# Order of five engines planned in eight passes instead of one, in a fused attention and mixer kernel

## Chip, cores and metric

One core of one Trainium2 chip. The metric is the device time of one execution in microseconds (us), lower is better. The kernel before takes 726.40 us (median of three runs, 725.94 to 727.46).

## The reference

Three layers follow each other on an array of 4 batches of 576 tokens with 512 channels: attention over a window of 128 tokens, a mixer with a low-rank product over tokens and a hidden layer of 2048, and a gated layer whose gate mixes tokens. All inputs and outputs are float32.

```python
def _attn_ref(q, k, v):                       # q, k, v: (4, 8, 576, 64)
    scores = scale * np.matmul(q, k.transpose(0, 1, 3, 2))
    mask = (rel >= 0) & (rel < 128)           # rel: distance of the two tokens
    scores = np.where(mask, scores + bias[None], -1000000000.0)
    scores = scores - np.max(scores, axis=-1, keepdims=True)
    attn = np.exp(scores)
    attn = attn / (np.sum(attn, axis=-1, keepdims=True) + 1e-09)
    return np.matmul(attn, v)

def _moe_ref(x, U, V, w_ch1, w_ch2):          # x: (4, 576, 512)
    h = x.transpose(0, 2, 1) @ U @ V
    u = x + h.transpose(0, 2, 1)
    return u + np.maximum(u @ w_ch1, 0.0) @ w_ch2

def _moe2_ref(x, w_in, w_spatial, b_spatial, w_out):
    h = np.maximum(x @ w_in, 0.0)
    u, v = (h[..., :512], h[..., 512:])
    v_n = (v - mean(v)) / np.sqrt(var(v) + 1e-06)
    v_s = np.einsum('ts,bsd->btd', w_spatial, v_n) + b_spatial[None, :, None]
    return (u * v_s) @ w_out
```

## The kernel before

Nothing is issued while the program is written down. Every step (a group of matmuls, an activation, a copy, a transfer) is a `Task` of the class `Plan`: the engines that may do it, its cost on each by a formula (`mm`, `dve`, `act`, `pool_tt`), the tasks it depends on, and a priority `prio`, a number that the author wrote beside the step. At the end `Plan.run` makes one pass forward in time: it takes the engine that is free first, gives it the ready task with the lowest `prio`, notes start and end by the formulas, and goes on. The order in which tasks were taken is the order in which every engine's instructions are then written, and each engine executes its own list strictly in order. The formulas thus set the order, never the time on the chip. A step with two ways (a multiplication on POOL or DVE, a copy on ACT or DVE) goes to the engine that takes it first.

TensorE's steps have a mode: full array (`None`), "quarters" (four matmuls of 64 rows and 64 columns side by side) or "quarter rows". When the mode of a PE task differs from that of the task before it, the plan adds 0.09 to its end.

The work in order of time:

- **Attention.** For each batch and each of four pairs of heads (`heads`, sixteen in all): scores (L911, quarters), the masked minimum on DVE (L922), the exponential on ACT (L927), the scaling by the row sum (L938 for the first batch; L947 on POOL or L949 on DVE for the others, nine a pair), 13 transposes of the weights (L957), copies out of PSUM (L376 on ACT, L377 on DVE), and the product with v (L995, quarters). SP loads q, k and v of each pair (L877, L888).
- **Low-rank mixing** of each batch: transposes of the attention's output (L1022), the product with U (L1038) and with V (L1051), and the sum on DVE (L1056). V's integer words are converted on DVE, and copied by four transfers (L859) of SP into the layout that L1051 wants.
- **Early groups.** The first quarter of the hidden layer, for three groups of 512 tokens (`early_group`), is woven into the attention: `first_of` (L505 to L507, 512 columns, PSUM bank `f1`) and `second` (L544 to L546, bank `acc`, four output blocks e = 0 to 3 one after the other). `collect` (L554) adds a block to the result and frees the bank. The ring `r_acc` has the one bank `acc`; the ring `r_a4` has the three `sc` banks of the scores and `acc`.
- **Rest of the hidden layer**: `first_of` and `second` with 384 columns, then `seven_group` (L766 to L768, L544 to L546), which makes each product of two-by-two blocks with seven multiplications. I call this the dense stage.
- **Gated layer** for each batch: `values_of` (L1273 to L1275), `gates_of` (L1349 to L1351, three banks X, Y and Z for each of i = 0 and 1, emptied by L1356 and L1360), the token mixing (L1393 to L1398), `outputs_of`, and the transfer of the result.

Of the kernel before, what the change touches and what calls it, by code (L numbers as in the profile page):

```python
# [11 lines left out]
F32 = mybir.dt.float32  # L12
# [128 lines left out]
    __slots__ = ("eng", "cost", "emit", "ways", "prio", "deps", "succ", "left", "before", "start", "lat", "port", "mode")  # L141


class Plan:


# [35 lines left out]
    def dma(self, p, n, emit, r=(), w=(), prio=0):  # L182

        self.add("SP", max(0.5, p * n * 4 / 235e3), emit, r=r, w=w, prio=prio, lat=2.6)

    def run(self):
        seq = {t: i for i, t in enumerate(self.tasks)}
        engines = sorted({e for t in self.tasks for e in t.ways})
        free = dict.fromkeys(engines, 0.0)
        port, mode = 0.0, None  # L190

        waiting = {e: [] for e in engines}
        ready = {e: ([], []) for e in engines}
# [26 lines left out]
        order = []  # L220
        while True:
# [14 lines left out]
            at, e = best  # L236
# [3 lines left out]
            if e in rival and choice:  # L240
# [3 lines left out]
                queue = min(choice)  # L244
                if queue is ready[e][1] and theirs and theirs[0][0] < queue[0][0]:
                    choice.remove(queue)
                    if not choice:
# [3 lines left out]
                        e = other  # L251
# [2 lines left out]
            queue = min(choice, default=None)  # L254
            if queue is None:
                continue
            t = heapq.heappop(queue)[2]
            t.start = at
            t.eng, t.cost, t.emit = t.ways[e]
            end = at + t.cost  # L260
            if e == "PE":
                end += 0.09 * (t.mode != mode)
                mode = t.mode
# [7 lines left out]
                if not s.left:  # L271
                    offer(s)
        assert len(order) == len(self.tasks)
        for t in order:
            t.emit()


def mm(n, m=128):
# [20 lines left out]
def tile_kernel(ctx, tc, qT, kT, v, U, V, w1, w2, w_in, wspT, bsp, w_out, bias, out):  # L299
# [212 lines left out]
        P.add("DVE", dve(n), lambda: nc.vector.scalar_tensor_tensor(  # L512
            out=hl.ap(), in0=src(), scalar=0.0, in1=f32(hh.ap()), op0=ALU.max, op1=ALU.subtract), r=r + [hh], w=[hl], prio=prio)

    def early_group(t0, n, wts, prio, evac):

        hs, ls = split_u(t0, n, evac, True)
        hid = []
        w = 512 // n
        for i in range(0, 4, w):  # L520
            f1 = r_f1.new([128, w, n], F32)
            for j in range(w):
                wt = wts[i + j][0]
                P.add("PE", 12 * mm(n), lambda f1=f1, j=j, wt=wt: first_of(f1[:, j], wt, hs, ls),
                      r=[p for x in hs + ls for p in x[2]] + [wt.part(0), wt.part(1)], w=[f1], prio=prio)
            hh, hl = r_h.new([128, w, n], F32R), r_h.new([128, w, n], F32R)
            leave_one(f1.ap, w * n, hh, hl, r=[f1], prio=evac)
            hid += [(hh, hl, j) for j in range(w)]
        for e in range(0, 4, w):
            es = tuple(range(e, e + w))  # L530
            acc = r_acc.new([128, w, n], F32)
            for i in range(4):
                second(wts, hid, i, es, acc, n, prio)
            collect(t0, n, es, acc, True, evac)
# [556 lines left out]

    done = 0
    for n in K["early"]:
        early_group(done, n, parts_w[0], 1e4 + done / 256, K["evac"])
        done += n

    r_xd, r_hl, r_c, r_t = (Ring(in_chan, tag, n, [end_att]) for tag, n in (("xd", 20), ("hl", 8), ("c", 6), ("t", 3)))
# [414 lines left out]
```

## Time and profile before

| What | Value |
|---|---|
| median of three runs | 726.40 us |
| the profiled execution | 726.64 us |
| its span | 724.84 us |
| PE busy | 708.5 us (98%) |
| DVE busy | 557.7 us (77%) |
| ACT busy | 331.7 us (46%) |
| POOL busy | 87.1 us (12%) |
| granted TensorE clock | 1.00 in every slice |
| chain that ended last, by engine | PE 87%, DVE 8%, ACT 2% |

PE's matmuls overlap, so a busy share near 100% can hide a slower pace: the pace is read from the starts of consecutive matmuls in the timeline. The span is 1.80 us shorter than the execution.

### The profile page before, as it was taken

The page shows a single profiled execution, that of the slowest core. Times are in us where ns is not written, and L with a number is a line of the kernel's source. Part 1 is how long each engine was busy: PE and PEld are TensorE (multiplying, and loading weights), DVE is VectorE, ACT ScalarE, POOL GpSimd, SP SyncE. Part 2 cuts the span into 40 slices and gives each one's busy share as a digit, 9 for nine tenths or more (in the row PEclk, how much of TensorE's full clock was granted, in tenths as well). Part 3 has the DMA queues.
Part 4 walks back from the last instruction along what each step waited for, and adds up shares of the span by engine and source line. Part 5 has one row for each costly group of instructions (what it writes and reads, how often), then busy time and mean ns, then how long its engine had stood idle before and what let it go on. Part 6 is the DMA issues. An engine that isn't in the chain of part 4 may idle for free.

```text
span 724.8 us, 14526 instructions
## 1 busy us (share of the span) xinstructions
PE 708.5 (98%) x5472; PEld 644.2 (89%) x5472; DVE 557.7 (77%) x1547; ACT 331.7 (46%) x904; POOL 87.1 (12%) x121
## 2 busy tenths in 40 slices
PE   7989999999999999999999999999999999999997
PEld 5657778778799999999999999999889898898896
DVE  5989997774597999999885997975599768368360
ACT  6977656564452635346042361432354524324212
POOL 1254221120400000000000000010342100100000
PEclk9999999999999999999999999999999999999999
DMA  9574312300064145727173253547631201100102
GB/s 266 184 256 139 97 49 82 92 16 2 1 213 164 56 164 190 229 88 244 50 233 100 90 207 114 161 135 266 211 140 42 74 26 50 64 11 1 58 1 73
DMA packets 53525, 84.07 MB, mean 116 GB/s; under 512 B 7504, under 2 KB 37712, under 8 KB 53456
## 3 DMA queue, kind: packets, MB, share of 16 engines
q1 hardware_dynamic: 53168, 82.86, 34.8%
q8 instruction: 43, 0.70, 0.4%
q10 hardware_dynamic: 288, 0.30, 0.1%
q14 instruction: 26, 0.21, 0.1%
HBM read 60.56 MB, written 22.28 MB: 114 GB/s over the span
## 4 chain that ended last, share of the span: by engine, by line
PE 87%; DVE 8%; ACT 2%; POOL 1%; issue 1%; DMA 1%; SPq 0%; ACTq 0%; POOLq 0%
PE sc L546 8%; PE sc L544 8%; PE sc L545 8%; PE at L767 6%; PE at L766 6%; PE at L768 6%; PE at L995 3%; PE sc L911 2%; PE at L957 2%; PE sc L1273 2%; PE sc L1275 2%; PE sc L1274 2%; PE acc L544 2%; PE acc L546 1%; PE acc L545 1%; DVE p L922 1%
## 5 line engine op out<-in xcount | busy, mean ns | idle before, releaser
L546 PE MATMUL sc<-hl,wa 128*128 128x384 f32 x320 | 108.8, 340 | 0.0
L544 PE MATMUL sc<-h,wa 128*128 128x384 f32 x320 | 107.5, 336 | 0.0
L545 PE MATMUL sc<-h,wa 128*128 128x384 f32 x320 | 107.4, 336 | 0.0
L927 ACT ACTIVATE p<-p,nmax 128x192 f32<-128x192 f32 (+1 forms) x144 | 61.7, 432 | 18.4 <-DVE nmax L922 18.2
L773 DVE TENSOR_TENSOR c<-at,c 128x384 f32<-128x384 f32 x90 | 50.0, 555 | 14.4 <-PE at L768 10.7
L766 PE MATMUL at<-xd,wa 128*128 128x384 f32 x180 | 60.8, 338 | 0.0
L768 PE MATMUL at<-xd,wa 128*128 128x384 f32 x180 | 60.8, 338 | 0.0
L767 PE MATMUL at<-xd,wa 128*128 128x384 f32 x180 | 60.8, 338 | 0.0
L546 PEld LDWEIGHTS sc<-hl,wa 128*128 128x128 f32 x320 | 60.1, 188 | 0.1
L544 PEld LDWEIGHTS sc<-h,wa 128*128 128x128 f32 x320 | 60.1, 188 | 0.0
L545 PEld LDWEIGHTS sc<-h,wa 128*128 128x128 f32 x320 | 60.0, 187 | 0.0
L811 DVE TENSOR_TENSOR y<-sc,y 128x384 f32<-128x384 f32 (+1 forms) x96 | 41.5, 456 | 24.0 <-PE sc L546 23.7
L922 DVE CUSTOM_DVE_ANT_0 p<-sc,bias 128x192 f32<-128x192 f32 (+1 forms) x144 | 40.8, 329 | 10.8 <-DMA bias<-in_bias 5.1
L376 ACT CAST wa<-st 128x256 fp32r<-128x256 f32 (+1 forms) x62 | 27.8, 475 | 31.6 <-DVE st L425 16.4
L911 PE MATMUL sc<-kr,qr 64*64 64x192 f32 (+2 forms) x576 | 33.3, 327 | 3.8 <-DMA kr<-in_kT 3.7
L778 ACT ACTIVATE h<-c 128x384 fp32r<-128x384 f32 x54 | 28.4, 526 | 14.1 <-DVE c L773 14.0
L563 POOL TENSOR_TENSOR t<-y 128x288 f32<-128x288 f32 x1 | 1.5, 1463 | 272.7 <-DVE y L811 272.7
L766 PEld LDWEIGHTS at<-xd,wa 128*128 128x128 f32 x180 | 33.8, 188 | 0.1
L767 PEld LDWEIGHTS at<-xd,wa 128*128 128x128 f32 x180 | 33.8, 188 | 0.0
L768 PEld LDWEIGHTS at<-xd,wa 128*128 128x128 f32 x180 | 33.8, 188 | 0.0
L957 PEld LDWEIGHTS at<-ident,p 128*128 128x128 f32 x208 | 23.4, 142 | 11.4 <-issue 2.8
L957 PE MATMUL at<-ident,p 128*128 128x128 f32 x208 | 31.6, 284 | 1.8 <-DVE p L949 0.8
(364 smaller groups left out, 1965.7 us busy)
## 6 DMA issues: line engine op xcount, KB each, us to landing
wa<-in_w SPq DMA_DIRECT2D x32, 512.0 KB, 5.0
xd<-formsa SPq DMA_DIRECT2D x24, 192.0 KB, 3.9
qr<-in_qT SPq DMA_DIRECT2D x15, 288.0 KB, 4.4
kr<-in_kT SPq DMA_DIRECT2D x15, 288.0 KB, 4.3
vr<-in_v SPq DMA_DIRECT2D x16, 256.0 KB, 3.6
raw<-in_w_in SPq DMA_DIRECT2D x8, 512.0 KB, 3.8
out<-h SPq DMA_DIRECT2D x15, 256.0 KB, 2.0
keptu<-raw SPq DMA_DIRECT2D x14, 256.0 KB, 2.4
```

Of the source, the lines that this page charges most:

```text
L544: nc.tensor.matmul(o, wt[:, 0, 0, c], hh[:, j], start=i == 0 and x == 0, stop=False, skip_group_check=True)
L545: nc.tensor.matmul(o, wt[:, 1, 0, c], hh[:, j], start=False, stop=False, skip_group_check=True)
L546: nc.tensor.matmul(o, wt[:, 0, 0, c], hl[:, j], start=False, stop=i == len(wts) - 1, skip_group_check=True)
L766: nc.tensor.matmul(o.ap(), wh()[:, k], xh.ap(), start=start and k == 0, stop=False, skip_group_check=True)
L767: nc.tensor.matmul(o.ap(), wl()[:, k], xh.ap(), start=False, stop=False, skip_group_check=True)
L768: nc.tensor.matmul(o.ap(), wh()[:, k], xl.ap(), start=False, stop=k == 1, skip_group_check=True)
L773: P.add("DVE", dve(N3), lambda: nc.vector.tensor_tensor(out=out.ap(), in0=ps_.ap(), in1=sb.ap(), op=ALU.add), r=[ps_, sb], w=[out], prio=0)
L811: P.add("DVE", dve(m), lambda acc=acc, dst=dst, s=s, m=m, o=o: nc.vector.tensor_tensor(out=dst[:, s : s + m], in0=acc[:, 0, o : o + m], in ...
L911: nc.tensor.matmul(s[o : o + 64, c0 : c0 + k1 - k0], qr[d, 64 * t : 64 * t + 64], kr[d, k0:k1], start=True, stop=True, skip_group_check=True)
L922: nc.vector.tensor_tensor_reduce(out=o(), in0=s[:, c0 : c0 + nk], in1=bias_t[:, pair, t % 2, 192 - nk :], scale=-0.125, scalar=BIG, op0=AL ...
L927: nc.scalar.activation(out=o(), in_=o(), func=AF.Exp, scale=-1.0, bias=nmax[:, sl, t : t + 1], accum_out=sums[:, sl, t : t + 1])
L957: P.add("PE", 0.109, lambda pt=pt, n_=n_, s0=s0: nc.tensor.transpose(pt[:, n_ - s0], p[:, n_ * 128 : n_ * 128 + 128], ident), r=[p.part(t) ...
```

## The change

`Plan.run` now makes eight rounds. In each, `forward` does what the one pass did; then `latest` walks the same tasks backward in time on the engines that they were given, and writes into each task's `prio` the negative of its distance from the end, so that the next round's forward pass takes first what must start first. The written priorities count in the first round alone. The plan with the smallest planned end of the eight is emitted. On PE, a ready task of the mode that is running is preferred to any other. The last early group's blocks e = 2 and 3 are summed in the ring `r_a4`, that is in two `sc` banks.

```diff
+PASSES = 8
@@ class Plan
+    def latest(self):
+        ahead, left = dict.fromkeys(self.tasks, 0.0), {t: len(t.succ) for t in self.tasks}
+        engines = sorted({t.eng for t in self.tasks})
+        free = dict.fromkeys(engines, 0.0)
+        waiting, ready = {e: [] for e in engines}, {e: [] for e in engines}
+
+        def offer(t):
+            heapq.heappush(waiting[t.eng], (ahead[t], -t.start - t.cost, self.seq[t], t))
+
+        for t in self.tasks:
+            if not left[t]:
+                offer(t)
+        for _ in self.tasks:
+            at, e = min((free[e] if ready[e] else max(free[e], waiting[e][0][0]), e) for e in engines if ready[e] or waiting[e])
+            while waiting[e] and waiting[e][0][0] <= at:
+                heapq.heappush(ready[e], heapq.heappop(waiting[e])[1:])
+            t = heapq.heappop(ready[e])[2]
+            free[e] = at + t.cost
+            t.prio = -free[e]
+            for d in t.deps:
+                gap = self.SAME.get(e, 0.13) if d.eng == e else self.CROSS
+                ahead[d] = max(ahead[d], free[e] + gap + d.lat)
+                left[d] -= 1
+                if not left[d]:
+                    offer(d)
+
     def run(self):
-        seq = {t: i for i, t in enumerate(self.tasks)}
+        self.seq = {t: i for i, t in enumerate(self.tasks)}
+        plans = []
+        for _ in range(PASSES):
+            order = self.forward()
+            plans.append((max(t.start + t.cost + t.lat for t in order), len(plans), [(t, t.eng, t.cost, t.emit, t.start) for t in order]))
+            self.latest()
+        for t, t.eng, t.cost, t.emit, t.start in min(plans)[2]:
+            t.emit()
+
+    def forward(self):
+        seq = self.seq
...
-            t = heapq.heappop(queue)[2]
+            if e == "PE":
+                live = [x for x in queue if not x[2].eng]
+                pick = min([x for x in live if mode and x[2].mode == mode] or live)
+                live.remove(pick)
+                queue[:] = live
+                heapq.heapify(queue)
+                t = pick[2]
+            else:
+                t = heapq.heappop(queue)[2]
...
-        for t in order:
-            t.emit()
+        return order
...
-    def early_group(t0, n, wts, prio, evac):
+    def early_group(t0, n, wts, prio, evac, spare):
...
-            acc = r_acc.new([128, w, n], F32)
+            acc = (r_a4 if spare and e > 1 else r_acc).new([128, w, n], F32)
...
-        early_group(done, n, parts_w[0], 1e4 + done / 256, K["evac"])
+        early_group(done, n, parts_w[0], 1e4 + done / 256, K["evac"], done + n == sum(K["early"]))
```

Most lines of the file move down by 47 (L505 becomes L552, L766 becomes L813, L1273 becomes L1320). Nearly every stretch of every engine's list changes in the attention; three places are shown, as the built programs have them.

**First, PE at the start of the program**, first two pairs of heads (`sc` scores, `at` transposes and products with v, `p_88` or `p_75` the first pair's attention weights). Before:

```order
L911 MATMUL sc<-kr,qr 64x192 x14
L957 MATMUL at<-ident,p_88 128x128 x13
L911 MATMUL sc<-kr,qr 64x64 x2
L911 MATMUL sc<-kr,qr 64x128 x2
L911 MATMUL sc<-kr,qr 64x192 x8
L995 MATMUL at<-ph,vr 64x64 x30
L995 MATMUL at<-ph,vl 64x64 x2
L968 MATMUL at<-y,ones 64x320 x2
L968 MATMUL at<-y,ones 64x256 x2
L911 MATMUL sc<-kr,qr 64x192 x6
```

Now:

```order
L958 MATMUL sc<-kr,qr 64x192 x14
L1004 MATMUL at<-ident,p_75 128x128 x4
L958 MATMUL sc<-kr,qr 64x64 x2
L958 MATMUL sc<-kr,qr 64x128 x2
L958 MATMUL sc<-kr,qr 64x192 x14
L1004 MATMUL at<-ident,p_75 128x128 x9
L1015 MATMUL at<-y,ones 64x320 x2
L1015 MATMUL at<-y,ones 64x256 x2
L1042 MATMUL at<-ph,vr 64x64 x30
L1042 MATMUL at<-ph,vl 64x64 x2
```

All the second pair's scores now stand behind four of the first pair's 13 transposes; before, they came behind all 13, and the last six of their rows behind the first pair's product with v.

**Second, SP around the four copies of the converted V** (`v_544`, `v_439`), which wait for DVE; `qr` and `kr` are the fifth pair's. Before:

```order
L406 DMA wa<-in_w 128x4x256
L406 DMA wa<-in_w 128x1024
L877 DMA qr<-in_qT 128x576
L877 DMA kr<-in_kT 128x576
L888 DMA vr<-in_v 128x2x256
L859 DMA v_544<-v_425 64x288 x4
L892 DMA vl<-in_v 64x8x64
```

Now:

```order
L453 DMA wa<-in_w 128x4x256
L924 DMA qr<-in_qT 128x576
L906 DMA v_439<-v_355 64x288 x4
L924 DMA kr<-in_kT 128x576
L935 DMA vr<-in_v 128x2x256
L453 DMA wa<-in_w 128x1024
```

The copies moved ahead of the fifth pair's `kr` and of the second weight load; their own sources are converted earlier in DVE's list than before (V now ahead of U).

**Third, PE at the first gates of the gated layer** (`wa,fg` and `wa,u`: values; `u,wa`: gates; `at`, `acc` and `f`: banks). Before:

```order
L1275 MATMUL at<-wa,fg 128x512
L1349 MATMUL at<-u,wa 128x288
...
L1351 MATMUL at<-u,wa 128x288
L1349 MATMUL acc<-u,wa 128x288
...
L1351 MATMUL acc<-u,wa 128x288
L1349 MATMUL at<-u,wa 128x288
```

Now:

```order
L1322 MATMUL f_6750<-wa,u 128x512
L1396 MATMUL at<-u,wa 128x288
...
L1398 MATMUL at<-u,wa 128x288
L1320 MATMUL at<-wa,fg 128x512
...
L1322 MATMUL at<-wa,fg 128x512
L1396 MATMUL acc<-u,wa 128x288
```

Twelve matmuls of the values (L1320 to L1322) moved from before the gates to between the gates' first twelve and the next; the same stands at all four batches.

## Rows read from the trace of the kernel before

**Rows 1.** The page, busy time of each engine over the span.

```profile
PE 708.5 (98%) x5472; PEld 644.2 (89%) x5472; DVE 557.7 (77%) x1547; ACT 331.7 (46%) x904; POOL 87.1 (12%) x121
```

**Rows 2.** Windows by stage: us, then PE, PEld, DVE, ACT, POOL busy, clock, DMA.

```profile
5.13:52.04 46.91, 41.61 (x698) 30.19 (x690) 40.52 (x176) 39.24 (x140) 15.19 (x14) 1.00 0.75 243
52.04:108.72 56.68, 55.47 (x675) 42.05 (x677) 54.80 (x202) 37.62 (x129) 17.80 (x24) 1.00 0.34 101
108.72:196.06 87.34, 86.16 (x1057) 66.96 (x1051) 55.15 (x215) 47.83 (x163) 17.69 (x30) 1.00 0.13 40
196.06:514.00 317.94, 317.94 (x1811) 317.39 (x1810) 269.99 (x620) 125.19 (x285) 5.84 (x8) 1.00 0.47 157
```

**Rows 3.** Timeline: DVE's first two tiles of scores that waited (start, us, idle before).

```profile
5.13 0.23 DVE L922 CUSTOM_DVE_ANT_0 p<-sc,bias 128x64 f32<-128x64 f32 x1 [5.13 <-DMA bias<-in_bias]
...
6.37 0.36 DVE L922 CUSTOM_DVE_ANT_0 p<-sc,bias 128x192 f32<-128x192 f32 x1 [0.52 <-PE sc L911]
```

**Rows 4.** Groups of instructions by form: the scaling on DVE and POOL, a conversion.

```profile
L949 DVE TENSOR_SCALAR p<-p,rinv 128x192 f32<-128x192 f32 x64 | 18.7, 351 | 0.0
L947 POOL TENSOR_TENSOR p<-p,rinv 128x192 f32<-128x192 f32 x20 | 10.4, 540 | 32.0 <-DVE rinv L935 28.0 <-DVE nmax L922 4.1
L425 DVE SCALAR_TENSOR_TENSOR st<-wa,st 128x512 uint32<-128x512 uint32 x32 | 22.3, 702 | 0.1
```

**Rows 5.** Timeline: a DVE conversion that started under a POOL subtraction.

```profile
53.19 1.36 POOL L563 TENSOR_TENSOR wa<-st,wa 128x512 fp32r<-128x512 f32 x1 [2.89 <-ACT wa L376]
...
54.13 0.96 DVE L425 SCALAR_TENSOR_TENSOR st<-wa,st 128x512 uint32<-128x512 uint32 x1
```

**Rows 6.** Timeline of PE: a full-array group after scores, and one before a product with v.

```profile
151.13 0.50 PE L505 MATMUL f<-x,wa 128*128 128x512 f32 x1
151.47 0.39 PE L506 MATMUL f<-x,wa 128*128 128x512 f32 x1
...
157.31 0.39 PE L545 MATMUL acc<-h,wa 128*128 128x512 f32 x1
157.53 0.40 PE L546 MATMUL acc<-h,wa 128*128 128x512 f32 x1
157.86 1.76 PE L995 MATMUL at<-ph,vr 128*64 128x64 f32 x60
```

**Rows 7.** Timeline of PE: the last early group, between two blocks.

```profile
189.26 0.39 PE L546 MATMUL acc<-h,wa 128*128 128x512 f32 x1
190.59 0.47 PE L544 MATMUL acc<-h,wa 128*128 128x512 f32 x1 [0.94 <-DVE y L554]
```

**Rows 8.** Timeline of PE: the first gates.

```profile
530.12 0.29 PE L1351 MATMUL acc<-u,wa 128*128 128x288 f32 x1
531.36 0.40 PE L1349 MATMUL at<-u,wa 128*128 128x288 f32 x1 [0.95 <-DVE y L1360]
...
533.74 0.29 PE L1351 MATMUL sc<-u,wa 128*128 128x288 f32 x1
534.23 0.40 PE L1349 MATMUL at<-u,wa 128*128 128x288 f32 x1 [0.19 <-DVE y L1360]
```

**Rows 9.** Timeline of SP's issues around the copies of V.

```profile
16.66 0.50 SPq L877 DMA_DIRECT2D kr<-in_kT  x1
20.52 0.38 SPq L888 DMA_DIRECT2D vr<-in_v  x1
26.79 2.89 SPq L859 DMA_DIRECT2D v<-v  x4
```

**Rows 10.** The page, DMA issues: count, KB each, median us to landing.

```profile
wa<-in_w SPq DMA_DIRECT2D x32, 512.0 KB, 5.0
...
kr<-in_kT SPq DMA_DIRECT2D x15, 288.0 KB, 4.3
```

**Rows 11.** Timeline of PE: fifth pair's scores, first early group, gated layer.

```profile
30.10 1.10 PE L911 MATMUL sc<-kr,qr 64*64 64x64 f32 x24
...
52.04 0.50 PE L505 MATMUL f<-x,wa 128*128 128x512 f32 x1
...
514.14 0.40 PE L1273 MATMUL sc<-wa,u 128*128 128x512 f32 x1
```

## The prediction

> **What bounds the kernel now.** I read the busy times of the page first, then the windows by stage, then the timeline of PE at the places where the new order differs. PE is busy for 98% of the span [rows 1], so the time can fall only where PE waits or where its pace is slower than its matmuls need. The windows say where that is [rows 2]. In the dense stage, 196 to 514 us, PE is busy in every one of the 317.94 us and its weight load in 317.39: there is nothing to gain, and whatever is won ahead of it simply moves it forward. Ahead of it lie two other cases. In the head, from DVE's first tile at 5.13 us to the first early group at 52.04, PE is idle for 5.3 of 46.91 us, and DVE is busy for 40.52 of them: the head is a chain of scores, minimum, exponential, transposes and copies, in which DVE has most of the work, and 6.4 us of DVE's time are lost to waits inside it. From 52 to 109 us DVE is busy for 54.80 of 56.68 us, so here DVE's own work counts. From 109 to 196 us DVE has 32 us to spare and PE is busy for 86.2 of 87.3: what is lost there is lost in changes of mode and in one wait for a bank. After 514 us the reader finds waits of PE only at the gates.
>
> **The change, part by part.**
>
> *The head (A).* The new list gives PE all of the second pair's scores behind four transposes of the first pair, where before 13 transposes and a product with v came ahead of the last of them. DVE then has the second pair's tiles to work on while the first pair's weights are turned. DVE's 6.4 idle us [rows 2] are the most that this can win; nothing at all is the least, since every pair still runs through the same chain. I take half, 3.2, because some of these waits cannot be reordered away: the first tile waits for a transfer until 5.13 and the fourth waits another 0.52 for scores whose own transfer now stands one place later on SP [rows 3].
>
> DVE also hands over work. I counted the scalings of attention weights in the two lists: 85 on DVE and 23 on POOL before, 74 and 34 now. Eleven at 0.351 us are 3.9 us of DVE [rows 4]. They are not all won, since a POOL instruction delays DVE: a conversion that started under a POOL subtraction took 0.96 us where its kind takes 0.702 on average [rows 4, 5], 0.26 more. Eleven times 0.26 is 2.9, so 1.0 us stays, and it counts, because DVE is nearly full until 109 us. The bounds are 3.9 (no delay) and a loss, which is a rival below. A is 3.2 + 1.0 = 4.2 us.
>
> The Trainium skill, in "SBUF — State Buffer", section "Who interferes with whom", says that a POOL instruction and a DVE instruction of certain kinds exclude each other for the whole length of the one that came first. By that rule the eleven moved scalings could hold DVE back for their whole length and the move would lose time; the delay in the trace, 0.26 us under an instruction of 1.36, is a part of a length, as one expects where the DVE instruction arrives late in it.
>
> *Changes of mode (B).* In the two lists PE changes its mode 103 times before and 77 times now up to the end of attention: 29 and 21 ahead of the first early group (these lie inside A), 74 and 56 after it. What one costs can be read from starts: inside an early group one matmul follows another after 0.22 us (157.31 to 157.53), but the last one before a product with v is followed after 0.33 (157.53 to 157.86), and the first one after scores after 0.34 (151.13 to 151.47) [rows 6]. So 0.11 us each way, and 18 fewer are 2.0 us. At the least they are worth nothing, if a step that was moved to save one now waits for its producer; at the most twice as much, 4.0, if a part of the price lies inside the small matmuls, where starts don't show it.
>
> *The last early group's banks (C).* Its third block had to wait for the bank `acc`: 189.26 to 190.59 is 1.33 us between two matmuls that otherwise follow after 0.22 [rows 7]. With `sc` banks for the blocks e = 2 and 3 this wait goes: 1.1 us. PE comes to the block 1.1 us earlier, and what could be late next is the `sc` bank, which low-rank mixing used last; so the bounds are 0 and 1.1. The 12 matmuls of 384 columns that stood between the third and the fourth block are only moved behind.
>
> *The gates (D).* PE waited 0.95 and 0.19 us there for DVE to empty a bank, and each time the next matmul took 0.40 us in place of 0.29 [rows 8]: 1.4 us in all. The new list puts twelve matmuls of the values between. They are the same matmuls, taken from ahead of the gates. The bounds are 0 and 1.4.
>
> *A new wait (E).* SP issues in order. The four copies of V wait for DVE, and they now stand ahead of the fifth pair's `kr` and of a weight load; before, SP stood still at them from 20.90 to 26.79 us [rows 9]. V is now converted about a pair earlier in DVE's list. Six pairs had their scores in the head's 46.9 us, 7.8 us a pair, so the conversion would be ready near 19 us, SP would issue the copies at 20.9 at the latest by its old pace, be done with them after 2.89, and `kr` would land 4.3 us after its issue [rows 9, 10]: at 28.1. The scores that need it ran at 30.10 [rows 11]; if the head is by then 3 us ahead, they are wanted at 27.1 and wait 1.0 us. If the conversion keeps its old time, `kr` lands at 34.0 and the wait is 6.9. I take 1.0, since the conversion's place did move. Behind the scores on PE stand the low-rank products and the first early group, so such a wait is paid in full.
>
> *At nothing.* The dense stage's lists differ little, and groups of `seven_group` are split by `second` of the group before. PE has no wait there now, and DVE with 270 of 318 us covers the reordering [rows 2]; what it costs if that cover is gone is the slower rival. Bits of work that moved between ACT and DVE (copies out of PSUM) I cost at nothing: ACT is busy for 39.24 of 46.91 us in the head and for two thirds after it. Nothing is added: the counts of matmuls, transfers and activations are the same.
>
> **The sum.** 4.2 + 2.0 + 1.1 + 1.4 - 1.0 = 7.7 us. The profiled execution took 726.64, which gives 718.9; it lies 0.24 above the median of the runs, so for that I forecast 718.7.
>
> **The rivals.**
>
> *The head keeps its time.* Then A and E are nothing, and B, C and D give 726.6 - 4.5 = 722.1 us. For it speaks that DVE is already busy for 86% of the head; against it that the waits of PE there come from many small causes, which an order can change. Chance 0.18.
>
> *POOL takes back more than it gives.* If each of the eleven scalings stops DVE for its 0.540 us [rows 4], DVE loses 5.9 us and wins 3.9: in place of +1.0 it is -2.0, and the time is 721.7. That is the result of the rule on SBUF named above. The trace shows shorter delays, so it gets 0.07.
>
> *The plan's gains come back as waits that its formulas do not see.* One late weight block in the dense stage is enough: a load takes 5.0 us to land [rows 10], and then four passes of at most 0.702 us [rows 4], 7.8 us together, and the time is 726.5, no change. The list now asks for these weights 6 us sooner. Against it: the loads wait for nothing but a buffer that the early groups free, and this moves forward too. Chance 0.07.
>
> *Slower.* The same mechanism twice: two blocks late by their whole 7.8 us give 734. It decides from 9.2 us of new waits in the dense stage. DVE has 48 us to spare there on average, which is why I give it only 0.08.
>
> *More.* If the head loses all its idle time and a change of mode costs twice what I read, A is 7.4, B 4.0, E 0, and the time is 726.6 - 13.9 = 712.7. Chance 0.06.
>
> **How the numbers follow.** The likeliest case, 0.54, is the sum. A measurement of this kernel can tell about 0.2%, 1.5 us, from no change. Faster by more than that (under 724.9) are the forecast, the first two rivals and the last, 0.54 + 0.18 + 0.07 + 0.06 = 0.85, less 0.03 for forecasts that fall short: 0.82. Same is 0.07 and a part of these, 0.09; slower is 0.09. The range must reach the cases at 722.1 and 712.7; to both sides I add what E and the bounds of A leave open: 712 to 726, which leaves out the slower case and the upper part of no change.
>
> **What the profile will show.** Right: the first 512-column matmul of the early groups (L552 then) starts near 48 us in place of 52.04, the first of the gated layer (L1320) near 508 in place of 514.14 [rows 11]; DVE is idle for less than 4 us between its first tile and the first early group; no wait on `acc` at the end of the last early group, and no wait of L1396 for L1407; the dense stage still 100% busy. Wrong: if the first early group starts at 52 again, A failed; if PE waits for `kr` at the fifth pair by more than 1 us, E was too small; if PE is idle between 190 and 508 us, the dense stage was starved; if the changes of mode still cost as much in total, B did. A first early group that starts earlier while L1320 does not would mean that DVE, not the order, sets the stretch from 52 to 109 us.

## The result and the profile after

The changed kernel takes 720.71 us (median of four executions, 719.92 to 722.00), the kernel before 726.69 beside it: a ratio of 0.9919, 95% interval 0.9901 to 0.9938. It is faster by 6.0 us or 0.8%, where 7.7 us were forecast. The profiled execution is the slowest of the four, 722.00 us, with a span of 720.2 us.

The page and the windows by stage of the changed kernel answer to [rows 1, 2] (columns as there; the last window is the gated layer):

```profile
PE 704.8 (98%) x5472; PEld 645.0 (90%) x5472; DVE 556.9 (77%) x1536; ACT 331.0 (46%) x906; POOL 93.2 (13%) x130
```

```profile
4.48:53.20 48.72, 41.86 (x657) 30.77 (x657) 42.21 (x179) 38.01 (x141) 14.45 (x13) 0.97 0.79 239
53.20:108.72 55.52, 53.91 (x708) 42.24 (x706) 52.70 (x190) 39.28 (x133) 23.12 (x29) 1.00 0.34 101
108.72:194.70 85.98, 85.64 (x1058) 67.42 (x1058) 55.16 (x211) 46.67 (x160) 19.71 (x36) 1.00 0.13 41
194.70:512.70 318.00, 318.00 (x1815) 317.96 (x1814) 271.31 (x622) 126.28 (x285) 5.80 (x8) 1.00 0.47 157
512.70:720.20 207.50, 204.25 (x1229) 186.15 (x1228) 135.56 (x337) 79.24 (x186) 28.38 (x30) 1.00 0.18 61
```

The dense stage is as rigid as before, busy in all of its 318 us. The head, from DVE's first tile to the first early matmul, has become longer (48.72 us against 46.91), and its mean clock is no longer 1.00. Three starts in the timeline of PE say where the time went; they answer to [rows 11], the middle one is the first matmul of `seven_group`:

```profile
53.20 0.60 PE L552 MATMUL f<-x,wa 128*128 128x512 f32 x1
...
228.50 0.34 PE L813 MATMUL at<-xd,wa 128*128 128x384 f32 x1
...
512.70 0.40 PE L1320 MATMUL sc<-wa,u 128*128 128x512 f32 x1
```

Before they stood at 52.04, 229.86 and 514.14. So the first early group comes 1.16 us later, `seven_group` 1.36 us earlier, the gated layer 1.44 us earlier, and the span ends 4.65 us earlier: 3.2 us of the gain lie in the gated layer (210.70 us before, 207.49 after), which the prediction gave 1.4. Ahead of the dense stage 6.3 us were forecast and 1.4 came in this execution. The median execution is 1.3 us faster than this one; in which stage is not shown.

The first early matmul is a weak mark, since the lists differ in what stands ahead of it (the fifth pair's product with v before, not after). The first matmul of `seven_group` has the same work ahead of it in every kernel here but for what is left over of the last groups, so I go by that one.

Four things are to be seen in the head of the changed kernel. First, its start. SP's issues, and DVE's first and fourth tile [rows 3]:

```profile
0.73 0.39 SPq L930 DMA_DIRECT2D qr<-in_qT  x1
1.18 0.42 SPq L1108 DMA_DIRECT2D bias<-in_bias  x1
1.64 0.43 SPq L930 DMA_DIRECT2D qr<-in_qT  x1
```

```profile
4.48 0.23 DVE L969 CUSTOM_DVE_ANT_0 p<-sc,bias 128x64 f32<-128x64 f32 x1 [4.48 <-PE sc L958]
...
7.83 0.36 DVE L969 CUSTOM_DVE_ANT_0 p<-sc,bias 128x192 f32<-128x192 f32 x1 [2.63 <-PE sc L958]
```

The bias is issued at 1.18 us (1.64 before) and DVE's first tile starts 0.65 us sooner, but the second part of the first `qr` is issued behind the bias, and then other transfers follow at once; the fourth tile starts at 7.83 in place of 6.37. Second, PE's waits in the head (engine, line, releaser: total us, times, longest):

```profile
PE sc L958 <- DMA qr<-in_qT: 1.8, 1, 1.8
PE sc L1098 <- ACT th L423: 1.3, 1, 1.3
PE sc L958 <- DVE nmax L969: 1.1, 1, 1.1
PE at L1004 <- DVE p L996: 1.0, 1, 1.0
PE at L1004 <- DMA qr<-in_qT: 0.5, 1, 0.5
PE at L1069 <- DVE u L1049: 0.4, 1, 0.4
PE at L1015 <- POOL y L985: 0.3, 1, 0.3
```

The wait for `kr` of the fifth pair (E) is not among them. Third, DVE under POOL, in the timelines of the two engines:

```profile
45.41 3.05 DVE L996 TENSOR_SCALAR p<-p,rinv 128x192 f32<-128x192 f32 x3
```

```profile
45.27 1.36 POOL L539 TENSOR_TENSOR x<-u,x 128x512 fp32r<-128x512 f32 x1 [0.51 <-ACT x L536]
46.59 0.52 POOL L994 TENSOR_TENSOR p<-p,rinv 128x192 f32<-128x192 f32 x1
47.07 1.28 POOL L539 TENSOR_TENSOR x<-u,x 128x512 fp32r<-128x512 f32 x1
```

Three scalings, whose usual duration is 0.31 us each, take 3.05 us together while POOL's instructions follow one another: 2.1 us of hold. Each of them starts after an instruction of POOL and ends 0.11 to 0.12 us after it (46.74, 47.23 and 48.47 us against 46.63, 47.11 and 48.35). The Trainium skill, "SBUF — State Buffer", section "Who interferes with whom", says that where an instruction of POOL and one of DVE of certain kinds meet, `tensor_scalar` on DVE among them, the later one is blocked for the whole length of the first; here the trace agrees with it. The price hangs on the length of POOL's instruction: the two scalings under a subtraction of 1.36 and 1.28 us lost 1.0 us each, the one under POOL's scaling of 0.52 us took 0.56 us and lost 0.25.

Fourth, the clock. Windows of 2 us, columns as above:

```profile
46.00:48.00 2.00, 0.99 (x9) 0.43 (x7) 2.00 (x3) 0.78 (x2) 2.00 (x3) 1.00 0.43 166
48.00:50.00 2.00, 0.88 (x14) 0.44 (x11) 2.00 (x14) 1.36 (x7) 0.35 (x1) 1.00 0.00 0
50.00:52.00 2.00, 2.00 (x21) 1.67 (x23) 2.00 (x10) 2.00 (x10) 0.00 (x0) 0.51 0.50 141
52.00:54.00 2.00, 2.00 (x19) 1.37 (x14) 2.00 (x8) 1.16 (x5) 0.07 (x1) 0.64 0.66 175
54.00:56.00 2.00, 2.00 (x11) 1.56 (x9) 2.00 (x9) 0.88 (x4) 2.00 (x3) 1.00 0.34 118
```

After a stretch in which PE was busy for less than half of the time, the granted clock stands at 0.5, the 1.2 GHz level, for 1.96 + 1.44 = 3.4 us (the values of two windows are mixtures of 0.5 and 1). I call this a drop. The head of the kernel before kept 1.00 in its profiled execution. The Trainium skill, "TensorE: Matmul & The Clock Gate", section "Part 1: The HAM clock gate", says that the clock has two levels and falls when the engine has been idle. The trace agrees on the two levels; ahead of this fall PE was not idle throughout but worked between five waits of 0.4 to 1.3 us (from 38 to 50 us).

At the end of the last early group the wait for `acc` is gone [rows 7]:

```profile
189.13 0.39 PE L593 MATMUL acc<-h,wa 128*128 128x512 f32 x1
189.35 0.39 PE L591 MATMUL sc<-h,wa 128*128 128x512 f32 x1
```

### The profile page after: what moved, and what is told of

Same layout as the page of the kernel before. It is cut to its first block, busy times and chain, and to the rows that moved or that the text cites. A ratio compares the mean times of both kernels' runs of the same rounds, so it can differ in the third digit from the quotient of the medians.

```text
span 720.2 us, 14536 instructions
## 1 busy us (share of the span) xinstructions
PE 704.8 (98%) x5472; PEld 645.0 (90%) x5472; DVE 556.9 (77%) x1536; ACT 331.0 (46%) x906; POOL 93.2 (13%) x130
## 4 chain that ended last, share of the span: by engine, by line
PE 91%; DVE 5%; DMA 2%; ACT 0%; issue 0%; SPq 0%; DVEq 0%; ACTq 0%
PE sc L593 8%; PE sc L591 8%; PE sc L592 8%; PE at L813 6%; PE at L814 6%; PE at L815 6%; PE at L1042 3%; PE at L1004 2%; PE sc L958 2%; PE sc L1320 2%; PE sc L1322 2%; PE sc L1321 2%; DMA vr<-in_v 2%; PE acc L591 2%; PE at L1322 1%; PE at L1321 1%
## 5 line engine op out<-in xcount | busy, mean ns | idle before, releaser
L591 PE MATMUL sc<-h,wa 128*128 128x384 f32 (+1 forms) x328 | 110.6, 337 | 0.0
L592 PE MATMUL sc<-h,wa 128*128 128x384 f32 (+1 forms) x328 | 110.5, 337 | 0.0
L974 ACT ACTIVATE p<-p,nmax 128x192 f32<-128x192 f32 (+2 forms) x144 | 61.6, 431 | 20.1 <-DVE nmax L969 20.1
L591 PEld LDWEIGHTS sc<-h,wa 128*128 128x128 f32 x328 | 61.6, 188 | 0.3
L592 PEld LDWEIGHTS sc<-h,wa 128*128 128x128 f32 x328 | 61.5, 187 | 0.3
L813 PE MATMUL at<-xd,wa 128*128 128x384 f32 x180 | 60.8, 338 | 0.0
L969 DVE CUSTOM_DVE_ANT_0 p<-sc,bias 128x192 f32<-128x192 f32 (+2 forms) x144 | 40.2, 326 | 12.3 <-PE sc L958 12.2
L958 PE MATMUL sc<-kr,qr 64*64 64x192 f32 (+2 forms) x576 | 34.9, 344 | 6.3 <-DMA kr<-in_kT 3.3
L813 PEld LDWEIGHTS at<-xd,wa 128*128 128x128 f32 x180 | 33.8, 188 | 0.0
```

Source lines behind the costliest of these rows:

```text
L591: nc.tensor.matmul(o, wt[:, 0, 0, c], hh[:, j], start=i == 0 and x == 0, stop=False, skip_group_check=True)
L592: nc.tensor.matmul(o, wt[:, 1, 0, c], hh[:, j], start=False, stop=False, skip_group_check=True)
L813: nc.tensor.matmul(o.ap(), wh()[:, k], xh.ap(), start=start and k == 0, stop=False, skip_group_check=True)
L958: nc.tensor.matmul(s[o : o + 64, c0 : c0 + k1 - k0], qr[d, 64 * t : 64 * t + 64], kr[d, k0:k1], start=True, stop=True, skip_group_check=True)
L969: nc.vector.tensor_tensor_reduce(out=o(), in0=s[:, c0 : c0 + nk], in1=bias_t[:, pair, t % 2, 192 - nk :], scale=-0.125, scalar=BIG, op0=AL ...
L974: nc.scalar.activation(out=o(), in_=o(), func=AF.Exp, scale=-1.0, bias=nmax[:, sl, t : t + 1], accum_out=sums[:, sl, t : t + 1])
```

## The experiments

Theory 1, from the two traces: the gain is made of gates, bank and changes of mode, and the planned head brings nothing. The rival: the new plan of the attention carries the gain. Twelve kernels ran in three sets (bank alone to head planned, no preference to filled, changed again to the last); each ratio is to the kernel before in the same set, and its medians there were 726.97, 727.56 and 726.60 us. In the second set six of the 13 executions of the kernel before had a mean clock of 0.997 or less, in the other two 3 of 17 and 3 of 11; so the ratios of the second set look better by about 0.001 (0.6 to 1.0 us), and I give medians beside them. The starts are those of the profiled executions, in us; "gated" is the time from the first values matmul to the end of the span, "drop" where the lower clock began in the head of that one execution.

| Kernel | Median | Ratio (95%) | first `seven_group` | gated | drop at |
|---|---|---|---|---|---|
| before | 726.6 to 727.6 | 1 | 229.86 | 210.70 | none |
| changed | 720.71 | 0.9919 (0.9901–0.9938) | 228.50 | 207.49 | 50 |
| bank alone | 725.63 | 0.9983 (0.9974–0.9991) | 229.93 | 210.67 | 43 |
| one pass | 724.42 | 0.9967 (0.9955–0.9979) | 228.44 | 210.44 | 47 |
| late part planned | 721.72 | 0.9930 (0.9917–0.9943) | 227.51 | 207.71 | none |
| head planned | 724.17 | 0.9958 (0.9942–0.9974) | 229.20 | 209.92 | 48 |
| no preference | 720.44 | 0.9898 (0.9876–0.9921) | 225.82 | 207.49 | none |
| start mended | 721.55 | 0.9909 (0.9885–0.9932) | 226.21 | 207.46 | none |
| no scaling on POOL | 724.68 | 0.9955 (0.9938–0.9971) | 231.51 | 207.49 | 50 |
| filled | 720.79 | 0.9900 (0.9878–0.9922) | 226.80 | 207.48 | none |
| changed again | 721.85 | 0.9921 (0.9903–0.9939) | 228.64 | 207.47 | 50 |
| late preference | 719.15 | 0.9891 (0.9874–0.9908) | 225.29 | 207.47 | none |
| late preference, start | 718.65 | 0.9886 (0.9870–0.9902) | 224.91 | 207.47 | 39 |
| filled, start | 719.91 | 0.9900 (0.9884–0.9917) | 226.42 | 207.51 | none |

**The bank alone**: the kernel before with the lines on `spare` of the change and nothing else.

> The kernel before with the spare bank alone: blocks e = 2 and 3 of the last early group are summed in two sc banks, one pass, written priorities. Theory 1 (the gain of the change is made of the gates, about 3 us, the bank, about 1 us, and the changes of mode, 1.5 to 2 us, and the head brings none): the wait of 1.33 us for acc near 190 us is gone, the first seven-multiplication matmul starts 1.1 us earlier than 229.86, the gated layer keeps its 210.7 us, the time falls by 1.1 us to about 725.5. Rival (the bank's wait is only passed on to the next bank or to DVE): 726.6, no change.

Measured: 0.9983, 1.2 us less. `seven_group` did not start earlier in the profiled execution, because this one had a drop of the clock at 43 us, so that its first early matmul stood at 53.35; from there to `seven_group` it took 176.58 us in place of 177.82. The bank is worth what C said.

**One pass**: the changed kernel with its own first pass only.

```diff
-PASSES = 8
+PASSES = 1
```

> The changed kernel with one pass, so with the written priorities; it keeps the preference for the running mode on PE and the spare bank. The list has 92 changes of mode in place of 103 (before) and 77 (changed). Theory 1: 11 changes of mode at 0.11 us and the bank's 1.1 us, together 2.3 us: 724.3 us; the gated layer still takes 210.7 us with its waits at the gates; no drop of the granted clock, first early matmul near 52. Rival (the passes alone make the gain, a preference only delays what is more urgent): 726 us or more.

Measured: 0.9967, 2.4 us less; bank and eleven changes of mode were to give 2.3. A drop came that was not expected, and the first early matmul stood at 53.53. The gated layer keeps its length, and a wait at the gates (the only one that the waits of PE after 500 us show):

```profile
PE at L1396 <- DVE y L1407: 1.3, 1, 1.3
```

**The late part planned, and the head planned**: derived priorities on one side only. The first edit is shown; the second keeps the written number where it is 1.5e4 or more.

```diff
             self.latest()
+            for t in self.tasks:
+                t.prio = written[t] if written[t] < 1.5e4 else 1e6 + t.prio
```

> Eight passes, but steps of the attention, the low-rank mixing and the early groups keep their written priorities; only the steps behind them (dense stage and gated layer) get the derived ones. Preference for the running mode and spare bank as in the changed kernel. Theory 1: the gated layer falls to about 207.5 us as in the changed kernel, the first early matmul stands near 52 us as before, no drop of the clock: 726.6 - 3.2 - 2.3 = 721.1 us, so nearly the whole gain without the planned head. Rival (the gates' waits went because the new attention leaves DVE less work behind, or the attention's plan brings the gain): gated layer 210 us and 724 us.

> The mirror of the run before: eight passes, derived priorities for attention, low-rank mixing and early groups, written ones for dense stage and gated layer; preference and spare bank as in the changed kernel. Theory 1: first early matmul at 53 and seven-multiplication matmul at 228.5 as in the changed kernel, gated layer back at 210.7 us with its waits for banks at the gates: 720.7 + 3.0 = 723.7 us. Rival: the time stays at 720.7.

Measured: with the late part planned the gated layer takes 207.71 us, all waits of PE after 500 us are gone, and the time is 0.9930, 5.2 us less. Against the one pass the gated layer wins 2.73 us. With the head planned it falls back to 209.92 us, and the time to 0.9958. So the gates' gain comes from the plan of the late steps and needs no new head. The head planned alone has the longest drop of all:

```profile
48.00:50.00 2.00, 1.44 (x11) 0.93 (x12) 2.00 (x14) 2.00 (x11) 0.00 (x0) 0.54 0.05 14
50.00:52.00 2.00, 2.00 (x22) 1.67 (x24) 1.71 (x7) 1.79 (x9) 0.00 (x0) 0.50 0.59 149
52.00:54.00 2.00, 2.00 (x16) 1.29 (x9) 2.00 (x7) 0.62 (x1) 0.43 (x1) 0.50 0.88 260
54.00:56.00 2.00, 2.00 (x8) 1.60 (x7) 2.00 (x9) 0.88 (x4) 2.00 (x3) 0.75 0.05 18
```

Its executions follow their clock: 721.88 and 722.51 us at a mean of 0.998, 723.97 and 724.37 at 0.997, 725.18 at 0.995, 725.73 at 0.993.

**No preference for the running mode**:

```diff
-            if e == "PE":
-                live = [x for x in queue if not x[2].eng]
-                pick = min([x for x in live if mode and x[2].mode == mode] or live)
...
+            t = heapq.heappop(queue)[2]
```

> The changed kernel without the preference for the running mode on PE: eight passes and the spare bank stay. 96 changes of mode in the list up to the end of attention (77 in the changed kernel, 103 before), and 11 scalings on POOL in place of 34. Theory 1 (gates 3.2 us, bank 1.1 us, 0.11 us for each change of mode): 726.7 - 3.2 - 1.1 - 0.8 = 721.6 us. Rival (the passes do no good without the preference, or the scalings that come back to DVE cost more than 2 us): 724 us or more.

Measured: 0.9898 and 720.44 us, where theory 1 had 721.6: 1.2 us better by the median, 2.3 by the ratio, with 19 changes of mode more than the changed kernel and 11 scalings on POOL in place of 34. `seven_group` starts at 225.82, 2.7 us ahead of the changed kernel, and the head shows no drop. The times alone do not tell it from the changed kernel (720.71 and 721.85). The starts speak against theory 1 in its part on the head: the passes do shorten it, and something that goes with the preference takes it back.

**The start mended**: SP's first eight issues as qr, qr, bias, vr, vl, then the second pair's.

```diff
+        at = [i for i, x in enumerate(plan) if x[1] == "SP"][:8]
+        for i, x in zip(at, [plan[at[j]] for j in (0, 2, 1, 6, 7, 3, 4, 5)]):
+            plan[i] = x
```

> The changed kernel with the first eight transfers of SP in another order and nothing else: both parts of the first qr, bias, vr, vl, then qr, kr and bias of the second pair. Theory 1 (the head lost at its start: the second part of the first qr landed at 6.2 us behind the bias): PE scores again near 4.8 us, DVE's fourth tile near 6.4 in place of 7.83, the first early matmul 1.4 us earlier than 53.20, 719.3 us. Rival (DVE's work or a later wait sets the end of the head, so what is won at the start is lost before 53 us): first early matmul at 53 again, 720.7 us.

Measured: 0.9909, not to be told from the changed kernel. DVE's fourth tile stands at 6.41 again, but the executions spread from 719.66 to 722.64 us with mean clocks from 0.992 to 1.0. For the start it is inconclusive by itself; the last two runs repeat it on other lists. For the clock it is telling: its profiled execution has the five waits of the changed kernel (0.42, 1.25, 0.54, 1.02 and 1.11 us) and no drop, and two more of its six executions had a mean clock of 1.0:

```profile
44.00:46.00 2.00, 0.98 (x11) 0.51 (x5) 2.00 (x3) 1.18 (x3) 2.00 (x3) 1.00 0.52 198
46.00:48.00 2.00, 0.89 (x14) 0.43 (x12) 2.00 (x12) 0.96 (x5) 0.74 (x1) 1.00 0.00 0
48.00:50.00 2.00, 1.94 (x33) 1.48 (x29) 2.00 (x12) 2.00 (x11) 0.00 (x0) 1.00 0.35 47
```

**No scaling on POOL**: the plan's order kept, each scaling that POOL had done by DVE at its place.

```diff
+            if t.eng == "POOL" and "DVE" in t.ways:
+                t.eng, t.cost, t.emit = t.ways["DVE"]
             t.emit()
```

> The changed kernel's plan, order as it is, with all 34 scalings that POOL had done by DVE at the same place of the order. It gives each scaling's worth on POOL. By the prediction (0.351 us of DVE saved, 0.26 lost to POOL's hold, 0.09 left): 34 x 0.09 = 3.1 us, 723.8 us. By the rule that each scaling on POOL holds DVE for its whole 0.540 us: DVE wins 6.4 us, the time falls to 720 or less. By theory 1, which reads from the changed kernel's trace that all scalings on POOL together held DVE for 3.1 us, 0.09 each: DVE gets 34 x 0.26 = 8.9 us more work, of which what lies before 110 us counts, so 725 us or more.

Measured: 0.9955 against 0.9919, 2.6 us slower than the changed kernel by the ratios, 2.8 to 4.0 by the medians (724.68 against 721.85 and 720.71); `seven_group` starts 3.0 us later. The 34 scalings are worth 0.08 to 0.12 us each on POOL. The prediction's 0.09 (0.351 less 0.26) fits, and a loss of 0.540 us for each is refuted: the time would have fallen. Theory 1's bound, 725 us or more, lies 0.3 us above the median and is not excluded.

**Filled**: 21 transposes of the identity more on PE in three of the head's waits; nothing reads their results.

```diff
+                        for _ in range(6 if (b, pair, n_) == (1, 0, 4) else 0):
+                            nc.tensor.transpose(pt[:, n_ - s0], ident, ident)
...
+                    if (b, pair, t) == (1, 1, 6):
+                        for _ in range(7):
+                            nc.tensor.transpose(s[:, 384:512], ident, ident)
...
+                for _ in range(8 if (b, pairs[0], sl.start) == (0, 2, 0) else 0):
+                    nc.tensor.transpose(outs[0][:, :128], ident, ident)
```

> The changed kernel with 21 transposes of the identity more on PE, whose results nothing reads: 8 ahead of the wait for th near 41.3 us, 6 ahead of the wait for p near 46.3, 7 ahead of the wait for nmax near 48.2; each lot takes at most 1.0 us and fits into its wait of 1.0 to 1.3 us. Theory 1 (the granted clock falls to 0.5 near 50 us because PE waited so much from 37 to 50 us, and costs about 1.7 us on the path): no drop, or a shorter one, clock 0.999 to 1.0, about 719.2 us. Rival 1 (the drop comes, but DVE is the bound there, so it costs nothing): no drop and still 720.7 us. Rival 2 (the drop does not hang on these waits): drop at the same place, 720.7 us or up to 1 us more.

Measured: the drop is gone. Windows of the filled kernel:

```profile
46.00:48.00 2.00, 1.77 (x13) 1.14 (x13) 2.00 (x7) 0.41 (x3) 1.30 (x2) 1.00 0.05 20
48.00:50.00 2.00, 1.79 (x20) 1.18 (x19) 2.00 (x14) 2.00 (x11) 0.00 (x0) 1.00 0.16 18
50.00:52.00 2.00, 1.96 (x24) 1.57 (x25) 2.00 (x6) 1.49 (x8) 0.00 (x0) 1.00 0.90 313
52.00:54.00 2.00, 2.00 (x10) 1.37 (x8) 2.00 (x11) 0.94 (x3) 1.12 (x2) 1.00 0.30 102
```

All six executions, and the five of the filled kernel with the mended start, had a mean clock of 1.0; of the ten executions of the changed kernel none was above 0.998. So work put into these waits keeps the clock: this is shown. That the waits alone make it fall is not: the kernel with the mended start had the same waits and kept its clock in three of six executions, and the late part planned, with a wait of 1.7 us at 48 us, in five of five. What decides between these cases is open.

What the drop costs is read best from the profiles, from the first `up` matmul after the wait for `th` to `seven_group`; the first line is of the changed kernel, the second of the filled one:

```profile
42.57 0.51 PE L1098 MATMUL sc<-v,th 32*128 32x288 f32 x1 [1.26 <-ACT th L423]
...
41.52 0.51 PE L1107 MATMUL sc<-v,th 32*128 32x288 f32 x1 [0.24 <-ACT th L423]
```

This stretch took 185.9 and 186.0 us in the two profiles of the changed kernel, with the drop, and 185.3, 185.3 and 185.2 in the two filled ones and the one with the mended start, without it: 0.6 to 0.75 us for 3.4 us at the lower clock. The rest of the filled kernel's earlier start lies ahead of the fill, where transfers landed sooner (PE's wait for `qr` was 1.1 us in place of 1.8). With the long drop of the head planned alone the same stretch took 187.38 us, 2.1 more. The times fit but do not show it: the median, 720.79 us, is what the rival "the drop costs nothing" had, and the ratio, 0.9900, is 1.4 us better than the changed kernel's, with overlapping intervals.

Theory 2 followed: the passes shorten the head, and the preference for the mode takes this back. The changed kernel and three others were run together.

> The changed kernel itself once more, beside the three that follow, as their measure: 720.7 us, a granted clock of 0.997 or 0.998 with the drop near 50 us, first early matmul near 53 us.

> The changed kernel, but the plan prefers the running mode on PE only from 45 us of its own time on, so in the head the most urgent step is taken whatever its mode. Up to the first early group PE's list is that of the run without the preference. 82 changes of mode in place of 77, 23 scalings on POOL in place of 34. Theory 2, formed from the run without the preference (the planned passes do shorten the head, by 3 us, and the preference for the mode takes this back and leaves the waits behind which the clock drops): first early matmul near 48.9 us, first seven-multiplication matmul near 224.5 to 225.5, no drop, 2 to 3.5 us less than the changed kernel, about 718 us. Rival (the run without the preference was faster for its fewer scalings on POOL or by chance of the list): first early matmul at 51 to 53, within 1 us of the changed kernel.

> The run before with SP's first eight transfers in the order of the run on the start (both parts of the first qr, bias, vr, vl, then the second pair's). Theory 2: the start gains some 0.6 us, as much as that run's first early matmul lay ahead of the filled run's (50.51 and 51.06 us, both without a drop): about 717.5 us. Rival (the head is set by DVE, so the start is worth nothing): the time of the run before.

> The changed kernel with both the 21 transposes that fill PE's waits and the mended start: the preference for the mode stays in the head. Theory 2: no drop of the clock in any run, first early matmul near 50.5, 2 us less than the changed kernel, 718.7 us, and 0.5 to 1 us slower than the two kernels with the late preference. Rival (the drop costs nothing since DVE is the bound): within 0.7 us of the changed kernel.

```diff
-                pick = min([x for x in live if mode and x[2].mode == mode] or live)
+                pick = min([x for x in live if mode and x[2].mode == mode and at > 45] or live)
```

Measured: the changed kernel is at 721.85 us, with the drop. The late preference is 2.7 us below it by the medians (0.9891 against 0.9921; the intervals overlap by 0.0005), and `seven_group` starts at 225.29, in the range that theory 2 gave. It has 23 scalings on POOL where the changed kernel has 34, which by the price above counts against it, so fewer scalings are not the cause. Its first early matmul stands at 50.87, not at 48.9: the fifth pair's product with v is ahead of it in this list. With the mended start as well it is 718.65 us, 0.9886, just clear of the changed kernel (0.9902 against 0.9903 at the near ends), although its profiled execution had a drop at 39 us. The start moved `seven_group` by 0.38 us in both pairs of lists (225.29 to 224.91, 226.80 to 226.42; the first pair with a drop in the second list only). The filled kernel with the start came 1.9 us below the changed one, 0.4 of it the start's, again with overlapping intervals. Between filled and late preference `seven_group` differs by 1.5 us in both pairs. The late preference with the mended start beats both kernels: 8.0 us below the one before and 3.2 below the changed one, in one set. The windows of the kernel with the late preference alone, head and then up to 108.72 us:

```profile
4.46:50.87 46.41, 42.21 (x722) 31.58 (x722) 40.27 (x178) 37.11 (x139) 11.15 (x9) 1.00 0.77 246
50.87:108.72 57.85, 56.45 (x668) 42.89 (x667) 55.90 (x206) 44.94 (x149) 19.80 (x24) 1.00 0.35 105
```

DVE still has 6.1 us idle in the head, as before: the plan did not take these waits away, it put more of PE's work under them (722 matmuls, where [rows 2] has 698 and the changed kernel 657).

## Why the prediction came out as it did

The time was in the range, 2.0 us above the forecast, but two errors of opposite sign met in it.

- **The head (A), +4.2 forecast: failed.** The step was that the new list lets DVE work through half of its 6.4 idle us. In the changed kernel DVE has 6.5 us idle in the head, and the sign of A having failed came, a first early group at 53.20. I read from the list that the second pair's scores come sooner, and did not ask what comes later: they start at 9.67 in place of 10.24 us, but the third pair's at 16.34 in place of 13.95, the fourth's at 22.31 in place of 20.77 and the fifth's at 30.78 in place of 30.10. This alone does not lose the head: with the late preference the third pair's are late too, at 15.07. Against the late part planned, which keeps the written head and starts `seven_group` at 227.51, the changed kernel is 1.0 us later and the late preference 2.2 us earlier. Taken out of the head, the preference for the running mode gives 2.7 us back by the medians and 3.2 at the start of `seven_group`. Of these 3.2 us 1.5 remain against the filled kernel, which has no drop; some 0.65 are the drop of the clock, which no step of the prediction had; and some 1.0 lie ahead of the fill, where the two profiles differ by their transfers, which is not the preference's doing as far as is shown. I had the bias and the second `qr` part in the rows of the start, and took the delay for small: at `seven_group` the start is worth 0.4 us.
- **The scalings within A, +1.0:** the price held. 34 of them on POOL are worth 2.6 to 4.0 us, so eleven 0.8 to 1.3. The rival's price, 0.540 us lost for each, is refuted; that DVE's instruction waits until POOL's has ended is what the trace shows, and it costs 1.0 us under a subtraction such as L539. Summing what DVE's instructions in the head took beyond the median of the same line and shape without POOL, while POOL ran, gives 0.6 us before and 3.3 after. No run isolated these 2.7 us, and the late preference has 2.3 of them too and is faster, so they are not shown to be on the path.
- **Changes of mode (B), 2.0, and the bank (C), 1.1: right in size as far as was run.** The bank alone gave 1.2 us. Bank and eleven changes together gave 2.4 where 2.3 were worked out. A change of mode alone was not run, nor the 18 of the sum.
- **The gates (D), +1.4: mis-sized.** I added the waits of the first batch [rows 8] and took the other three to have none, because the waits' rows name only these. Counted from the starts of the gates' matmuls, against their median pitch of 0.133 us, the loss was 1.9, 0.7, 0.3 and 0.3 us in the four batches, 3.2 in all, and is 0.65 after. The gated layer won 2.7 us with the late part planned (against the one pass) and 3.2 in the changed kernel; of the 3.2, 0.4 is the tail behind the last matmul (3.66 to 3.23 us).
- **The wait for `kr` (E), -1.0: did not come.** V was later than the sum had it, the copies at 22.91 and not at 20.9, `kr` at 25.40 and not at 23.8. By the sum's own 4.3 us to landing that is 29.7 us; the scores that need it stood at 30.78, since the head was not 3 us ahead but 0.7 behind. So the term fell with A:

```profile
22.91 2.44 SPq L906 DMA_DIRECT2D v<-v  x4
25.40 0.58 SPq L924 DMA_DIRECT2D kr<-in_kT  x1
...
30.78 1.10 PE L958 MATMUL sc<-kr,qr 64*64 64x64 f32 x24
```

- **At nothing:** the dense stage stayed at 284.2 to 284.3 us from `seven_group` to the values in every profile. The rival of late weight blocks did not come.

The rival "the head keeps its time", 722.1 us, described the head of the changed kernel; the gates' 1.8 us more made the time look like the forecast. That the number came so near was luck. Open are what lets the clock fall in one execution and not in another, and whether POOL's subtractions cost time in the head.

## What to carry to other kernels

When a planner is changed, switch its parts on one at a time: here the derived priorities won at the gates, a preference beside them lost in the head what they could have won there, and a preference that began only behind the head kept the gain. What it adds behind the head over none at all, 0.5 us at `seven_group` (225.82 to 225.29), is not clear of the noise. Size a wait that repeats per batch from the pitch of the instructions in each batch, not from the listed waits of the first. Before leaving short waits on TensorE alone because another engine is the bound, look at the granted clock behind them.

## What the hardware showed that I had not expected

Behind scattered waits of 0.4 to 1.3 us each in 12 us of the head, with PE busy for 0.9 to 1.6 of every 2 us, the granted clock stood at 0.5 for 3.4 us, and for 6.8 us in another profile (1.84 + 2 + 2 + 1.0, from the four windows of the head planned). Twenty-one transposes, started some 0.11 us apart and put into three of these waits, kept it at 1.00 in eleven of eleven executions, where none of the changed kernel's ten kept it. The same waits did not always bring the fall: with another order of the first transfers three of six executions had none. The kernel before is close to the same edge: of its 41 executions beside these runs, 12 had a mean clock of 0.997 or less. In the third set these took 727.8 to 729.3 us, where the others took 726.4 to 727.2; in the second, where the mean fell as low as 0.990, 728.4 to 731.8 against 726.5 to 727.6. So executions of one kernel with and without such a fall lay 1 to 5 us apart.
